# Another order for the first quarter of an attention and MoE kernel: casts with heads outermost, some joint for q and k

## The chip, the cores and the metric

The kernel runs on one core of a Trainium2 chip. The metric is device time in microseconds (us). Engines are PE (matmuls; its weight loads are listed as PEld), DVE (vector), ACT (scalar), POOL (general) and SP (which only issues transfers here). Each engine works through its instructions in the order in which they stand in its program and waits on semaphores for the others.

## The reference

Attention with a fixed mask per head, then a gated two-layer product.

```python
scores = scale * np.matmul(q, k.transpose(0, 1, 3, 2))       # 4 batches, 8 heads, 768 x 64
stream_keep = causal & (is_sink | in_win)                    # 4 sink keys, a window of 64
mask = np.where(retr[0, :, 0, 0, None, None], full_mask, stream_mask)   # heads 0, 2, 6: plainly causal
a = np.exp(scores - max);  a = a / (sum(a) + 1e-09);  attn = np.matmul(a, v)
x = attn.transpose(0, 2, 1, 3).reshape(3072, 512)
h = x @ w_in                                                 # 512 x 2048
g = h * (1.0 / (1.0 + np.exp(-beta * h)))
out = g @ w_out                                              # 2048 x 512
```

## The kernel before

The 3072 rows are worked in eight chunks of 384 rows (a batch and one of its halves), each chunk in four units of two heads: 32 units. For a unit the kernel casts k and q from float32 to bf16 (L246), turns them on PE (L326), copies them from PSUM to tiles KT and QTD (L334 for k, L337 for q), multiplies them (L455) on top of a mask that PE adds (L426), takes exp on ACT (L464), and multiplies with v (L536). v is cast into VX (L251), and the four sink keys and values go into tiles KO and VO (L316, L259, L260), both copied by POOL. DVE normalizes (L545, L549). PE turns the result (L574, copied to xT at L583), multiplies it with w_in (L604); ACT takes tanh (L609), DVE makes the gate (L612), and PE multiplies with w_out (L657).

The program's order is written out by hand. The first eight units (chunks 0 and 1) follow RAMP, a string of words that are carried out one after the other; the rest follows PLAN, likewise a string, which stands as it is. In a word the letters are the step, the number is the unit (for loads, values and rows of x: the chunk or tile), and the last letter the engine: v is DVE, a is ACT, g is POOL.

- ck, cq: the cast of k or q of a unit. tk, tq: its three transposes on PE. kk, kq: the copy to KT or QTD. ko: the sink keys.
- ad, qk, ex, ma: mask, scores, exp and mask product of a part of a unit (ex0.1 is the second part of unit 0). cv: the cast of a v tile. vo: the sink values. pv, no: the product with v and the normalization.
- xx, cx: the transposes of x and the copy to xT. hm, mm, mA: first products of the MoE part. mb: second products, four matmuls each. be: beta's transpose.
- lq, lv: loads of q and k, and of v, issued by SP (L119, L132); with a g they are held back by a small memset on POOL (L115, L129). Chunk 0's first loads are issued in front of RAMP: unit pairs 0 and 1 into one tile, 2 and 3 into another, k and q apart. wi, wo: the four loads of w_in and of w_out, issued by POOL (L140, L144). ro, rk, rq: row loads for later chunks, issued by POOL (L282).
- zz: matmuls with a tile of zeros (L517) that keep PE at work; idle(9) does the same in front of RAMP (L167).

The staging tiles of k and q and of v are two of each kind, so the loads of chunk 2 fill the tiles of chunk 0.

Of the kernel before, what the change touches and what calls it, by code (L numbers as in the profile page):

```python
# [18 lines left out]
def kernel(  # L19
# [82 lines left out]

    staged = {}

    def load_qk(c, g, pairs=1, held=False):

        b, h2 = chunks[c]
        rows = slice(h2 * HALF, (h2 + 1) * HALF)  # L110
        both = stage.tile([128, 2, 4, HT, D], F32, name=f"s{g}")
        for i, (name, src) in enumerate((("k", k), ("q", q))):
            staged[name, c, g] = both[:, i]
            if held:
                nc.gpsimd.memset(staged[name, c, g][:, 0, 0, 0:1], 0.0)  # L115
        for i in range(pairs):
            for name, src in (("k", k), ("q", q)):
                eng = nc.scalar if g == 0 and pairs == 2 and name == "q" else nc.sync
                eng.dma_start(  # L119
                    out=staged[name, c, g][:, i:4:pairs].rearrange("p h t d -> p h (t d)"),  # L120
                    in_=src[b, 4 * g + i:4 * g + 4:pairs, rows, :].rearrange("h (p t) d -> p h (t d)", t=HT))
# [20 lines left out]
    def load_w_out(i):  # L142
        f = slice(i * 4, (i + 1) * 4)
        nc.gpsimd.dma_start(out=w_out_sb[:, f, :], in_=moe_w_out.rearrange("(fo fi) d -> fi fo d", fi=128)[:, f, :])  # L144
        w_done.add(i)

    load_qk(0, 0, 2)
    load_qk(0, 1, 2)
    warm = consts.tile([1, 1], F32, name="warm")
# [7 lines left out]
    nc.vector.memset(zeros, 0.0)  # L157
# [6 lines left out]
    def idle(n, pool, name):  # L164
        for i in range(n):
            nothing = pool.tile([128, 512], F32, name=name)
            nc.tensor.matmul(nothing, zeros[:, 0:128], zeros, start=True, stop=True)  # L167
# [63 lines left out]
    def masks_late(h2):  # L231

        m = Mh[h2]
        if h2 == 0:
            return [lambda: nc.vector.tensor_copy(out=m[:, 3:5], in_=m[:, 1:3])]
        return [lambda i=i: nc.vector.tensor_copy(out=m[:, i:i + 2 * HT - 1:2], in_=Mh[0][:, i + 1:i + 2].to_broadcast([128, HT, 128]))
                for i in range(2)]


    def cast(u, name, copy):  # L240
        b, h2, p = units[u]
        c = u // NPAIR
        s = st_u.setdefault(u, {})
        if "qkb" not in s:
            s["qkb"] = att.tile([128, 2, HT, 2, D], BF16, name="qkb", bufs=4)
        copy(out=s["qkb"][:, "qk".index(name)], in_=staged[name, c, p // 2][:, p % 2:4:2].rearrange("p h t d -> p t h d"))  # L246

    def cast_v(c, t, copy):

# [39 lines left out]
    def transposes_dma(c, names=("k", "q")):  # L289
# [12 lines left out]
        for u in range(c * NPAIR, (c + 1) * NPAIR):  # L302
            p = u % NPAIR
            st_u[u] = {"QT": QT[:, place[p], :]}

    def sinks_of(u):
# [12 lines left out]
        copy(out=ko[:, ka - 1:kz - 1, 0:64], in_=kt[:, None, 0:64].to_broadcast([128, n, 64]))  # L319

    def transpose_qk(u, name):

        s = st_u.setdefault(u, {})
        tp = ps_m.tile([128, 512], F32, name="mm").bitcast(BF16)[:, 0:HALF].rearrange("p (t j) -> p t j", t=HT)
        for t in range(HT):
            nc.tensor.transpose(tp[:, t, :], s["qkb"][:, "qk".index(name), t].rearrange("p h d -> p (h d)"), ident)  # L326
        s["t" + name] = tp

    def copy_qk(u, name, copy):
# [56 lines left out]
    def steps_QK(u):  # L386
# [86 lines left out]
                        part(i)  # L473
            return (56 * sum(len(tiles[i][0]) for i in some) + 250, go)

        def mask(i):
            ev = views[i]
            ms = [[x for x, e in enumerate(tiles[i][r]) if e[5] is not None] for r in range(2)]
            if ms[0] and ms[0] == ms[1]:
                n = len(ms[0])  # L480
                m0 = tiles[i][0][0][5]
                nc.vector.tensor_mul(ev[:, :, 0:n], ev[:, :, 0:n], Mh[h2][:, None, m0:m0 + n].to_broadcast([128, 2, n, 128]))  # L482
            else:
                for r in range(2):
# [29 lines left out]
    def keep_busy(n):  # L514

        for i in range(n):
            nc.tensor.matmul(sums_bank(0), zeros[:, 0:128], zeros, start=True, stop=True)  # L517

    def steps_PV(u):
        b, h2, p = units[u]  # L520
# [180 lines left out]
    def do(word):  # L701
# [2 lines left out]
        n, i = int(n or 0), int(i or 0)  # L704
        if what in ("ck", "cq"):
            cast(n, what[1], copies[eng])
        elif what in ("tk", "tq"):
            step((170, lambda: transpose_qk(n, what[1])))
        elif what in ("kk", "kq"):
# [3 lines left out]
        elif what in ("ad", "qk", "ex", "ma"):  # L713
            if n not in visits:
                visits[n] = steps_QK(n)
            step((0 if what in ("ex", "ma") else 170, lambda: visits[n][what](i)))
        elif what == "cv":
            cast_v(n, i, copies[eng])
        elif what == "vo":
# [19 lines left out]
        elif what == "be":  # L739
            step((100, beta_go))  # L740
        elif what == "lv":
            load_v(n, held=eng == "g", tiles=[i])
        elif what == "lq":
            load_qk(n, i, held=eng == "g")
        elif what == "wi":
            load_w_in(n)
        elif what == "wo":
            load_w_out(n)
        elif what == "rq":
            rows_queries()  # L750
        elif what == "rk":
            rows_keys()
        elif what == "ro":
            if n not in more_rows:
                more_rows[n] = load_rows(n)
            more_rows[n].pop(0)()
        elif what in ("dk", "dq"):
            transposes_dma(n, what[1])
        elif what == "ml":
            late[n].pop(0)()  # L760
        elif what == "tt":
            run(steps_T(n))
        elif what == "zz":
            keep_busy(n)
        elif what == "hm":
            opened.append(done[0])
            done[0] += 1
            step(halves[0](opened[-1], 0))
        elif what == "hf":
            step(halves[0](opened.pop(0), 1))  # L770
        else:
            feed({"mm": "a", "mA": "A", "mb": "b"}[what])

    def feed(x):
# [16 lines left out]
        kq1v tk1 kk1v lq1.0g be qk0.1 ex0.0 zz3 ad1.0 cv0.0g ko1 lq1.1 ex0.1 pv0 ck3v cq3g tk3 lv1.0g cq2a tq2 kk3v  # L791
        lv1.1 cv0.1g ad1.1 qk1.1 kk2v ex1.1 tq3 ko2 qk1.0 wi0 vo0 cq4g lv1.2 cv0.2a lq2.0g ko3 pv0 kq2v pv0 ad2.0
        qk2.0 lv2.0 ex1.0 pv1 kq3a pv1 ck4v ad2.1 qk2.1 lv2.1 pv1 ex2.0 ad3.0 tq4 no0 tk4 ex2.1 ck7g kk4a qk3.0 ad3.1
        qk3.1 no1 pv2 ck6v ex3.0 cq5v ck5g pv2 tk6 xx0 ad4.0 cq6g pv3 kq4v ex3.1 pv2 ad4.1 cx0v ad5.0 qk4.1 pv3 lv2.2
        no2 on1g tq5 pv3 qk4.0 kk6a ml0 tk5 cq7g kq5v ex4.1 kk5a ko5 ko6 ad5.1 tq6 wi1 qk5.0 ex4.0 tk7 tq7 ex5.0 no3
        qk5.1 ex5.1 kq6v xx1 ad6.0 kk7v wi2 kq7v wi3 cx1a qk6.0 ml1 ad6.1 ex6.0 cv1.1g ko7 qk6.1 cv1.0v ex6.1 hm lq2.1
        ma5.0 ma5.1 mm cv1.2g vo1 mm wo0 pv4 lv3.0g ad7.0 lv3.1 pv4 hf pv4 no4 qk7.0 ad7.1 pv5 pv5 ex7.0 lv3.2 qk7.1
        pv5 no5 ml1 wo1 ex7.1 pv6 pv6 wo2 mm pv7 rq pv7 pv7 no7 wo3 pv6 no6 rk cq8g xx2 ro3 cx2a mA mA ck8g xx3 cx3a
        mm mA mm mA mm mm mA mm mm mm mA mm ro3 mm mm mA mm mm mm ro3 mA mm ro3 mA mm ro3 mm mm ro3 mA mA mb mb tt8 mb
# [116 lines left out]
```

## Time and profile before

| what | us |
|---|---|
| median of the runs shown (228.56 to 230.24) | 228.68 |
| the profiled execution's own time | 229.6 |
| its span, from the first to the last instruction | 227.7 |
| PE busy | 219.3 (96%) |
| ACT busy | 154.0 (68%) |
| DVE busy | 141.5 (62%) |
| POOL busy | 87.0 (38%) |
| the chain that ended last | PE 92% |

A row of the timeline gives the start and the length in us, the engine, the line of the kernel, the operation with output and inputs, how many instructions the row holds, and in brackets the idle time of the engine just before it with what ended it. A row of a group gives busy time and the mean duration in ns. A row of a transfer gives its size and the time from issue to landing. The profiled execution is one of several, and 0.9 us longer than the median.

### The profile page before, as it was taken

The page shows a single profiled execution, that of the slowest core. Times are in us where ns is not written, and L with a number is a line of the kernel's source. Part 1 is how long each engine was busy: PE and PEld are TensorE (multiplying, and loading weights), DVE is VectorE, ACT ScalarE, POOL GpSimd, SP SyncE. Part 2 cuts the span into 40 slices and gives each one's busy share as a digit, 9 for nine tenths or more (in the row PEclk, how much of TensorE's full clock was granted, in tenths as well). Part 3 has the DMA queues.
Part 4 walks back from the last instruction along what each step waited for, and adds up shares of the span by engine and source line. Part 5 has one row for each costly group of instructions (what it writes and reads, how often), then busy time and mean ns, then how long its engine had stood idle before and what let it go on. Part 6 is the DMA issues. An engine that isn't in the chain of part 4 may idle for free.

```text
span 227.7 us, 5023 instructions
## 1 busy us (share of the span) xinstructions
PE 219.3 (96%) x1898; PEld 126.4 (56%) x1917; DVE 141.5 (62%) x342; ACT 154.0 (68%) x254; POOL 87.0 (38%) x143
## 2 busy tenths in 40 slices
PE   7799999999999999999999999999999999999993
PEld 2456766654555665555644665556645665456553
DVE  4479988872584679347932689447964769038600
ACT  2588899846866898358943897669875877138521
POOL 5286952239254359543049209940260000000000
PEclk9999999999999999999999999999999999999998
DMA  6999999999999799989769977799804030110012
GB/s 197 233 319 239 222 197 199 194 222 165 168 207 150 176 155 113 157 191 143 96 137 147 163 173 99 90 140 153 219 4 123 8 81 0 49 62 30 0 51 91
DMA packets 95384, 31.67 MB, mean 139 GB/s; under 512 B 81776, under 2 KB 92416, under 8 KB 95360
## 3 DMA queue, kind: packets, MB, share of 16 engines
q1 hardware_dynamic: 58880, 22.82, 50.3%
q0 software_dynamic: 35904, 8.13, 41.6%
q10 hardware_dynamic: 576, 0.40, 0.6%
q8 instruction: 15, 0.25, 0.5%
q14 instruction: 9, 0.07, 0.1%
HBM read 27.27 MB, written 6.29 MB: 147 GB/s over the span
## 4 chain that ended last, share of the span: by engine, by line
PE 92%; DMA 2%; POOL 1%; ACT 1%; issue 1%; DVE 0%; SPq 0%; ACTq 0%
PE mm L657 35%; PE mm L604 25%; PE sp L604 12%; PE sp L455 7%; PE po L536 6%; DMA s<-in_k_dram 2%; PE mm L642 2%; PE mm L326 2%; PE sp L426 1%; PE mm L574 1%; PE mm L455 1%; PE mm L536 1%; DVE KT L334 0%; ACT qkb L246 0%; SPq L119 0%
## 5 line engine op out<-in xcount | busy, mean ns | idle before, releaser
L657 PE MATMUL mm<-w_out_sb,gT 128*128 128x512 bf16 x349 | 84.0, 379 | 1.3 <-issue 0.5
L464 ACT ACTIVATE es<-sp 128x768 bf16<-128x768 f32 (+2 forms) x72 | 56.5, 837 | 19.3 <-PE sp L455 19.1
L604 PE MATMUL mm<-xT,w_in_sb 128*128 128x384 bf16 x348 | 64.6, 326 | 0.0
L604 PEld LDWEIGHTS <-w_in_sb 128*128 128x128 bf16 x512 | 47.8, 98 | 29.7 <-issue 0.2
L609 ACT ACTIVATE th<-mm,beta_h 128x384 f32<-128x384 f32 x87 | 49.8, 588 | 5.8 <-PE mm L604 1.1
L657 PEld LDWEIGHTS <-gT 128*128 128x128 bf16 x368 | 33.4, 98 | 36.0 <-issue 1.5
L612 DVE SCALAR_TENSOR_TENSOR gT<-th,mm 128x384 bf16<-128x384 f32 x87 | 46.7, 551 | 6.9 <-ACT th L609 3.2
L604 PE MATMUL sp<-xT,w_in_sb 128*128 128x384 bf16 x164 | 32.3, 326 | 0.0
L251 POOL CAST VX<-vs 128x512 bf16<-128x512 f32 x16 | 10.1, 628 | 55.6 <-DMA vs<-in_v_dram 52.2
L661 ACT ACTIVATE osb<-mm 128x512 f32<-128x512 f32 x23 | 13.9, 602 | 25.5 <-PE mm L657 25.2
L536 PEld LDWEIGHTS <-es 128*128 128x128 bf16 x472 | 23.5, 98 | 12.9 <-issue 1.3
L612 DVE SCALAR_TENSOR_TENSOR gT<-th,sp 128x384 bf16<-128x384 f32 x41 | 22.3, 552 | 5.6 <-ACT th L609 3.6
L609 ACT ACTIVATE th<-sp,beta_h 128x384 f32<-128x384 f32 x41 | 23.8, 586 | 2.2 <-PE sp L604 0.2
L536 PE MATMUL po<-VX,es 128*128 128x65 bf16 x360 | 24.9, 194 | 0.4 <-ACT VX L251 0.4
L282 POOL DMA_DIRECT2D s<-in_k_dram x30 | 22.4, 757 | 7.3 <-DMA w_out_sb<-in_moe_w_out_dram 5.2
L282 POOL DMA_DIRECT2D s<-in_q_dram x30 | 22.4, 774 | 5.2 <-DMA w_out_sb<-in_moe_w_out_dram 5.2
L545 DVE RECIPROCAL rec<-po 128x6 f32<-128x6 f32 x28 | 5.4, 192 | 27.6 <-PE po L536 27.5
L455 PE MATMUL sp<-QTD,KT 64*128 64x128 bf16 (+2 forms) x258 | 19.2, 240 | 1.7 <-ACT QTD L337 1.4
L482 DVE TENSOR_TENSOR es<-es,Mh 128x768 bf16<-128x768 bf16 (+1 forms) x26 | 17.0, 683 | 5.0 <-ACT es L464 4.4
L549 DVE TENSOR_TENSOR x<-po,rec 128x384 bf16<-128x384 f32 x28 | 15.6, 557 | 1.0
L455 PEld LDWEIGHTS <-KT 64*128 64x128 bf16 x278 | 11.1, 94 | 6.9 <-issue 4.7
L259 POOL COPY VO<-VX 128x512 bf16<-128x512 bf16 x16 | 10.0, 648 | 7.4 <-DVE VX L251 7.4
(74 smaller groups left out, 157.1 us busy)
## 6 DMA issues: line engine op xcount, KB each, us to landing
vs<-in_v_dram SPq DMA_DIRECT2D x24, 256.0 KB, 5.8
out_dram<-osb SPq DMA_DIRECT2D x23, 256.0 KB, 2.8
w_in_sb<-in_moe_w_in_dram POOLq DMA_DIRECT2D x4, 512.0 KB, 9.5
w_out_sb<-in_moe_w_out_dram POOLq DMA_DIRECT2D x4, 512.0 KB, 16.6
s<-in_k_dram POOLq DMA_DIRECT2D x30, 64.0 KB, 4.3
s<-in_q_dram POOLq DMA_DIRECT2D x30, 64.0 KB, 5.9
s<-in_k_dram SPq DMA_DIRECT2D x4, 384.0 KB, 6.6
s<-in_q_dram SPq DMA_DIRECT2D x4, 384.0 KB, 8.2
```

The costliest lines, as they stand in the source:

```text
L251: copy(out=VX[b % 2][:, h2 * HT + t, :, 0:D], in_=staged["v", c][:, t])
L282: nc.gpsimd.dma_start(out=ROWS[c % 2, name][:, t, i * 4 * D:(i + 1) * 4 * D].rearrange("p (h d) -> p h d", d=D), in_=src[b, i:H:2, r:r + 1 ...
L455: nc.tensor.matmul(sps[i][r][:, x * 128:y * 128], key(a, lhs), s["QT"][half(a), qi * 128:(qi + y - x) * 128], start=first, stop=first or y ...
L464: nc.scalar.activation(out=views[i].rearrange("p r k j -> p r (k j)"), in_=banks[2][:, :, 0:n * 128], func=ACTF.Exp, scale=scale)
L482: nc.vector.tensor_mul(ev[:, :, 0:n], ev[:, :, 0:n], Mh[h2][:, None, m0:m0 + n].to_broadcast([128, 2, n, 128]))
L536: nc.tensor.matmul(po[:, qi, hh, :], e, val, start=(j == 0), stop=(j == len(lst) - 1))
L549: nc.vector.tensor_mul(xg[g][:, :, :, u % 2, :].rearrange("p a t d -> p t a d"), po[:, :, :, 0:D], rec.to_broadcast([128, HT, 2, D]))
L604: nc.tensor.matmul(hp[:, 0:HALF], w_in_sb[:, mo, fi * 128:(fi + 1) * 128], xT[c][:, mo, :], start=(mo == 0), stop=(mo == MO - 1))
L609: nc.scalar.activation(out=th, in_=hp[:, 0:HALF], func=ACTF.Tanh, scale=beta_h[:, fi:fi + 1])
L612: nc.vector.scalar_tensor_tensor(out=gTs[c][:, fi, :], in0=th, scalar=1.0, in1=hp[:, 0:HALF], op0=ALU.add, op1=ALU.mult)
L657: nc.tensor.matmul(op, gTs[c][:, fi, ns * 128:(ns + 1) * 128], w_out_sb[:, fi, :], start=(fi == 0), stop=(fi == FO - 1))
L661: nc.scalar.activation(out=osb, in_=op, func=ACTF.Copy, scale=0.5)
```

## The change

Five things change.

1. The tile of zeros is 128x128 where it was 128x512; a filler matmul streams it four times over by a broadcast. It is set first on DVE. idle(9) goes, and the word zi4 takes its place.
2. The casts of k and q read and write heads outermost; k stands ahead of q in the unit's tile.
3. cast_both casts k and q of one unit in one instruction of 768 elements per partition. Its words are cb0g, cb3a, cb4g, cb7g and cb5v, so five units use it. (Functions for transposes and copies of two units at once are defined, and no word uses them.)
4. Mask products and late masks can name an engine; the words in use leave them on DVE.
5. RAMP is another string: other engines for casts and copies, another order of loads, and another order on every engine.

```diff
-    zeros = consts.tile([128, 512], BF16, name="zeros")
+    zeros = consts.tile([128, 128], BF16, name="zeros")
+    still = zeros[:, None, :].to_broadcast([128, 4, 128])
...
-            nc.tensor.matmul(nothing, zeros[:, 0:128], zeros, start=True, stop=True)
-    idle(9, ps_m, "mm")
+            nc.tensor.matmul(nothing.rearrange("p (n j) -> p n j", n=4), zeros, still, start=True, stop=True)
...
-        copy(out=s["qkb"][:, "qk".index(name)], in_=staged[name, c, p // 2][:, p % 2:4:2].rearrange("p h t d -> p t h d"))
+        copy(out=s["qkb"][:, "kq".index(name)].rearrange("p t h d -> p h t d"), in_=staged[name, c, p // 2][:, p % 2:4:2])
...
+    def cast_both(u, copy):
+        c, p = u // NPAIR, u % NPAIR
+        s = st_u.setdefault(u, {})
+        s["qkb"] = att.tile([128, 2, HT, 2, D], BF16, name="qkb", bufs=4)
+        copy(out=s["qkb"].rearrange("p i t h d -> p i h t d"), in_=both_of[c, p // 2][:, :, p % 2:4:2])
...
     RAMP = """
-        ck0g ne1 lv0.0 lv0.1 tk0 ck2a ne0 cq0v ck1a zz3 tq0 kq0a zz3 ad0.0 on0v lv0.2 kk0v cq1v tq1 qk0.0 tk2 ad0.1
+        zi4 ad0.0 zz2 ne1 cb0g ck1a lv0.0 ne0 lv0.1 tq0 cq1g on0v tk0 lv0.2 kq0v lq1.0g zz2 kk0a tq1 tk1 ck2a qk0.0
+        ex0.0 lq1.1 ad0.1 zz5 qk0.1 be ad1.1 cb3a kk1v ex0.1 zz2 cq2a tk2 kk2v ko1 cv0.0g zz1 zz1 tk3 ad1.0 tq3
...
+        cq8g lv3.1 no5 ml1 pv6 pv6 pv6 no6 ex7.0 ex7.1 mm wo1 pv7 pv7 xx2 lv3.2 pv7 ck8g cx2a mA mA mm wo2 rq no7
```

Three places show how instructions move. The first is ACT, from its first cast on: L246 and L251 before, L248 and L312 after, are the casts (L312 the joint one), the COPY rows are those from PSUM to KT and QTD, and es is an exp. Before:

```order
L246 CAST qkb<-s_92 128x384
L246 CAST qkb<-s_87 128x384
L337 COPY QTD_144<-mm 128x384
L464 ACTIVATE es<-sp 128x768 x2
L246 CAST qkb<-s_92 128x384
L464 ACTIVATE es<-sp 128x512
L251 CAST VX_145<-vs 128x8x64
```

and after the change:

```order
L248 CAST qkb<-s_89 128x2x3x64
L361 COPY KT_131<-mm 128x384
L248 CAST qkb<-s_94 128x2x3x64
L491 ACTIVATE es<-sp 128x768
L312 CAST qkb<-s_94 128x2x2x3x64
L491 ACTIVATE es<-sp 128x768
L248 CAST qkb<-s_94 128x2x3x64
L364 COPY QTD_126<-mm 128x384
L491 ACTIVATE es<-sp 128x512
```

Unit 1's cast stands first and unit 2's third, the copy between them is that of unit 0's k, and a joint cast (unit 3, second staging tile) stands between the first two exps; the cast of a v tile is no longer ACT's.

The second place is POOL, where it issues the w_out loads, with the casts of unit 8 (staging tile s_293 before, s_312 after). Before:

```order
L251 CAST VX_146<-vs 128x8x64
L259 COPY VO_148<-VX_146 128x8x64
L260 COPY VO_148<-VX_146 4x8x64
L144 DMA w_out_sb<-in_moe_w_out_dram 128x4x512
L129 MEMSET vs 128x3
L144 DMA w_out_sb<-in_moe_w_out_dram 128x4x512 x3
L246 CAST qkb<-s_293 128x384
```

and after the change:

```order
L145 DMA w_out_sb<-in_moe_w_out_dram 128x4x512
L253 CAST VX_128<-vs 128x8x64
L130 MEMSET vs 128x3
L261 COPY VO_130<-VX_128 128x8x64
L262 COPY VO_130<-VX_128 4x8x64
L116 MEMSET s_599 128x1 x2
L248 CAST qkb<-s_312 128x2x3x64
L145 DMA w_out_sb<-in_moe_w_out_dram 128x4x512
L248 CAST qkb<-s_312 128x2x3x64
L145 DMA w_out_sb<-in_moe_w_out_dram 128x4x512 x2
```

The first w_out load moved ahead of the v cast, and the others behind the casts of unit 8: cq8g between the first and the second, ck8g between the second and the third.

The third place is SP's queue of loads, from chunk 1's v (the rows of three) to chunk 2's second half (s_293 and s_539 before, s_312 and s_599 after). Before:

```order
L132 DMA vs<-in_v_dram 128x8x64 x3
L119 DMA s_293<-in_k_dram 128x4x192
L119 DMA s_293<-in_q_dram 128x4x192
L132 DMA vs<-in_v_dram 128x8x64 x3
L119 DMA s_539<-in_k_dram 128x4x192
L119 DMA s_539<-in_q_dram 128x4x192
```

and after the change:

```order
L133 DMA vs<-in_v_dram 128x8x64 x4
L120 DMA s_312<-in_k_dram 128x4x192
L120 DMA s_312<-in_q_dram 128x4x192
L133 DMA vs<-in_v_dram 128x8x64 x3
L120 DMA s_599<-in_k_dram 128x4x192
L120 DMA s_599<-in_q_dram 128x4x192
```

One v load moved ahead of each pair of k and q.

More of the change, by code (lines that the diff above doesn't have):

```diff
@@ L145, in load_w_out @@
         w_done.add(i)
+    zeros = consts.tile([128, 128], BF16, name="zeros")
+    nc.vector.memset(zeros, 0.0)
+    still = zeros[:, None, :].to_broadcast([128, 4, 128])
     load_qk(0, 0, 2)
@@ L516, in keep_busy @@
         for i in range(n):
-            nc.tensor.matmul(sums_bank(0), zeros[:, 0:128], zeros, start=True, stop=True)
+            nc.tensor.matmul(sums_bank(0).rearrange("p (n j) -> p n j", n=4), zeros, still, start=True, stop=True)
     def steps_PV(u):
@@ L706, in do @@
             cast(n, what[1], copies[eng])
+        elif what == "cb":
+            cast_both(n, copies[eng])
+        elif what in ("wk", "wq"):
+            step((340, lambda: transpose_two(n, what[1])))
+        elif what in ("yk", "yq"):
+            copy_two(n, what[1], copies[eng])
         elif what in ("tk", "tq"):
@@ L715, in do @@
                 visits[n] = steps_QK(n)
-            step((0 if what in ("ex", "ma") else 170, lambda: visits[n][what](i)))
+            if what == "ma":
+                step((0, lambda: visits[n][what](i, engines[eng or "v"])))
+            else:
+                step((0 if what == "ex" else 170, lambda: visits[n][what](i)))
         elif what == "cv":
@@ L759, in do @@
         elif what == "ml":
-            late[n].pop(0)()
+            late[n].pop(0)(copies[eng or "v"])
         elif what == "tt":
             run(steps_T(n))
+        elif what == "zi":
+            idle(n, ps_m, "mm")
         elif what == "zz":
@@ L795 @@
[L795 to L799, printed above, removed]
@@ new lines @@
+        ko6 tk5 pv3 cx0a tq5 ex4.1 on1g no2 ad5.1 kk5a ad5.0 ko5 qk4.0 kq5a pv3 tq6 wi1 no3 qk5.0 wi2 tk7 kq6v tq7
+        qk5.1 ex4.0 ex5.0 xx1 ex5.1 kk7v ml1 kq7a ad6.0 qk6.0 hm wi3 ad6.1 ko7 cx1v wo0 qk6.1 ex6.0 ex6.1 mm ad7.0
+        cv1.1g cv1.0v ma5.1 hf pv4 ma5.v cv1.2v pv4 mm pv4 ad7.1 lv3.0g vo1 pv5 qk7.0 no4 qk7.1 pv5 rk lq2.1g pv5
+        cq8g lv3.1 no5 ml1 pv6 pv6 pv6 no6 ex7.0 ex7.1 mm wo1 pv7 pv7 xx2 lv3.2 pv7 ck8g cx2a mA mA mm wo2 rq no7
+        xx3 mA cx3v wo3 mm ro3 mm mm mA mm mm mm mA mA mm mm mA ro3 mm mm mA ro3 mm mm ro3 mm mA mm ro3 mm mm ro3 mA
@@ L801 @@
+        mA mb mb tt8 mb mb mb
     """
```

44 lines of the change are left out of this document (29 added, 15 removed).

## The prediction

> **What bounds the kernel now.** I read the page's shares and chain first, then the busy time by stretch, then the rows of single engines.
>
> ```profile
> PE 219.3 (96%) x1898; PEld 126.4 (56%) x1917; DVE 141.5 (62%) x342; ACT 154.0 (68%) x254; POOL 87.0 (38%) x143
> PE 92%; DMA 2%; POOL 1%; ACT 1%; issue 1%; DVE 0%; SPq 0%; ACTq 0%
> 0.00:5.00 5.00, 3.71 (x12) 1.33 (x13) 1.86 (x8) 1.49 (x2) 3.25 (x15) 1.00 0.59 179
> 20.00:25.00 5.00, 4.96 (x54) 2.98 (x55) 4.87 (x9) 5.00 (x8) 4.89 (x10) 1.00 1.21 243
> 30.00:50.00 20.00, 19.95 (x125) 11.74 (x124) 16.37 (x31) 16.48 (x29) 7.34 (x11) 1.00 1.25 202
> ```
>
> The columns of a stretch are its length, then the busy time of PE, PEld, DVE, ACT and POOL, and behind them the granted clock (1.00). From 30 to 50 us PE is busy 19.95 of 20 and the chain is 92% PE: behind the ramp the kernel is a row of matmuls, and the change leaves these in place. So a gain can come only from the first 25 us, and only if PE reaches the same matmul sooner. In 20 to 25 us PE, DVE, ACT and POOL are all nearly full, ACT with 5.00 of 5. The PE waits of that part:
>
> ```profile
> 1.29 3.59 PE L167 MATMUL mm<-zeros 128*128 128x512 bf16 x9 [1.29 <-DVE zeros L157]
> 5.02 0.81 PE L517 MATMUL po<-zeros 128*128 128x512 bf16 x3
> L517 PE MATMUL po<-zeros 128*128 128x512 bf16 x9 | 2.4, 380 | 0.0
> 8.46 0.34 PE L455 MATMUL sp<-QTD,KT 64*128 64x128 bf16 x4 [1.40 <-ACT QTD L337]
> 13.18 0.31 PE L536 MATMUL po<-VX,es 128*128 128x65 bf16 x5 [0.40 <-ACT VX L251]
> 15.40 0.34 PEld L326 LDWEIGHTS <-qkb 128*128 128x128 bf16 x6 [0.34 <-POOL s L115]
> 20.04 0.34 PE L455 MATMUL sp<-QTD,KT 64*128 64x256 bf16 x4 [0.25 <-ACT KT L334]
> ```
>
> The largest is 1.40 us ahead of the first scores at 8.46; the three behind it add 0.40 + 0.34 + 0.25 = 0.99. That is all the named waiting there is to win: 2.39 us, 1.0% of the time. (About 1% is what a measurement of this kernel can tell from no change.)
>
> **The start.** What releases the first scores now:
>
> ```profile
> 7.11 0.92 ACT L246 CAST qkb<-s 128x384 bf16<-128x384 f32 x2 [3.74 <-DMA s<-in_k_dram]
> 7.94 0.47 ACT L337 COPY QTD<-mm 128x384 bf16<-128x384 bf16 x1
> 8.84 0.81 ACT L464 ACTIVATE es<-sp 128x768 bf16<-128x768 f32 x1 [0.43 <-PE sp L455]
> 9.94 0.81 ACT L464 ACTIVATE es<-sp 128x768 bf16<-128x768 f32 x1 [0.29 <-PE sp L455]
> 3.93 0.41 POOL L187 TENSOR_SCALAR_AFFINE_SELECT Nc<-Nc 128x256 bf16<-128x256 bf16 x1
> s<-in_q_dram SPq DMA_DIRECT2D x1, 192.0 KB, 5.0
> L246 POOL CAST qkb<-s 128x384 bf16<-128x384 f32 x8 | 4.1, 525 | 2.2 <-PE sp L604 1.4 <-PE mm L326 0.4 <-DMA s<-in_q_dram 0.3
> L246 ACT CAST qkb<-s 128x384 bf16<-128x384 f32 x3 | 1.4, 507 | 3.7 <-DMA s<-in_k_dram 3.7
> L251 POOL CAST VX<-vs 128x512 bf16<-128x512 f32 x4 | 2.5, 628 | 5.3 <-DMA vs<-in_v_dram 5.3
> L251 ACT CAST VX<-vs 128x512 bf16<-128x512 f32 x1 | 0.6, 612 | 0.0
> ```
>
> Before, ACT takes unit 2's cast ck2a first, whose k lands at about 7.1; behind it stand the cast of unit 1 and kq0a, the copy that the first scores need. The change puts kq0 on DVE, and unit 0's k and q into one POOL cast of 768 elements. No row shows such a cast. From 384 elements in 525 ns and 512 in 628 ns, an element more costs 0.80 ns, so I take 628 + 256 x 0.80 = 833 ns; the same step on ACT (507 and 612) gives 822. The ends: no shorter than the 628 of 512 elements, no longer than two single casts, 1,050. POOL is free at 3.93 + 0.41 = 4.34, so cb0g ends at about 5.2, the copies kq0v and kk0a follow the transposes, and I put the first scores at about 6.65: 1.8 us earlier than 8.46.
>
> Almost none of that lasts. The first exp (L464) now stands behind ck2a, whose data still land at 7.1, so it starts at 7.1 + 0.5 = 7.6 instead of 8.84. Next on ACT is cb3a, the joint cast of unit 3: it waits for **both** loads, and the q of that pair is issued at 3.95 and lands 5.0 later, at 8.95. It runs 8.95 to 9.8, and ex0.1 stands behind it. ex0.1 starts at 9.7, where it started at 9.94. The head start of 1.8 is 0.2 at this point; the five fillers (zz5) ahead of its scores lie in the same wait and cost nothing.
>
> **From 10 to 24 us: ACT.** Between ex0.1 and the first tanh at about 24 the two orders differ on ACT as follows:
>
> ```profile
> L337 ACT COPY QTD<-mm 128x384 bf16<-128x384 bf16 x2 | 1.0, 476 | 0.0
> 12.02 0.60 ACT L464 ACTIVATE es<-sp 128x512 bf16<-128x512 f32 x1 [0.88 <-PE sp L455]
> 15.96 0.48 ACT L334 COPY KT<-mm 128x384 bf16<-128x384 bf16 x1 [0.33 <-PE mm L326]
> 18.45 0.81 ACT L464 ACTIVATE es<-sp 128x768 bf16<-128x768 f32 x1 [0.44 <-PE sp L455]
> 23.83 1.23 ACT L609 ACTIVATE th<-mm,beta_h 128x384 f32<-128x384 f32 x2
> ```
>
> Gone are cv0.2a (0.61) and kk6a (0.48); new are kq1a, kq5a and kq7a (3 x 0.48 = 1.44); cx1a and cx0a are the same work. ACT gets 1.44 - 1.09 = 0.35 us **more** to do and starts it 0.2 earlier. If its idle time stays where it is, the first tanh comes 0.15 later. Its larger idle times in between were 0.88 + 0.33 + 0.44 = 1.65. If all of that closed up, the tanh would come 1.5 earlier. I take the first end, nearer to the rows, because landings still hold the middle:
>
> ```profile
> s<-in_q_dram SPq DMA_DIRECT2D x1, 384.0 KB, 4.9
> 15.30 0.13 POOL L115 MEMSET s<- 128x1 f32 x2
> ```
>
> Chunk 1's q is issued at 9.86 and lands 4.9 later, at 14.75, whatever stands ahead. Before, k and q of unit 4 were cast apart and POOL's half was done at 15.3 (the memset that follows it); the joint cb4g starts at 14.75 and takes 0.83, so tq4, at 15.41 before, starts at about 15.6 or 15.7: 0.25 later. The wait at 13.18 for the third value tile goes, since cv0.2 moves to the DVE, but what it won is waited for at tq4. I carry **+0.1** to the first tanh and from there to the end; ends -1.5 and +0.35.
>
> Costed at nothing: heads outermost in the casts on ACT and POOL (same elements) and DVE (off the path, since kk and kq copies follow by PE's transposes); the narrow zero tile (the matmul streams the same 512 columns); fillers, which fill waits. Should a filler stand where PE no longer waits it costs (0.81 - 0.38) / 2 = 0.215 each (the row of 5.02 and the mean of its group, 380 ns), four of them 0.9. cv1.2 on the DVE behind mask products takes the value copies of POOL with it; it frees 0.63 of POOL, and stays inside the full stretch of DVE, at most 0.45 later.
>
> **The weights.** This is the one place where the change adds a wait in front of a queue. POOL issues the four w_out loads one behind the other; afterwards the cast cq8g stands between the first and the second, and it needs the q of chunk 2, which SP now issues behind one more v load.
>
> ```profile
> 25.42 0.75 POOL L144 DMA_DIRECT2D w_out_sb<-in_moe_w_out_dram  x1
> 26.19 2.24 POOL L144 DMA_DIRECT2D w_out_sb<-in_moe_w_out_dram  x3
> 29.88 0.51 POOL L246 CAST qkb<-s 128x384 bf16<-128x384 f32 x1 [1.45 <-PE sp L604]
> w_out_sb<-in_moe_w_out_dram POOLq DMA_DIRECT2D x1, 512.0 KB, 12.7
> w_out_sb<-in_moe_w_out_dram POOLq DMA_DIRECT2D x1, 512.0 KB, 20.6
> 19.54 2.01 SPq L119 DMA_DIRECT2D s<-in_q_dram  x1
> s<-in_q_dram SPq DMA_DIRECT2D x1, 384.0 KB, 10.2
> vs<-in_v_dram SPq DMA_DIRECT2D x1, 256.0 KB, 14.7
> w_in_sb<-in_moe_w_in_dram POOLq DMA_DIRECT2D x1, 512.0 KB, 8.8
> 48.91 1.46 PE L657 MATMUL mm<-w_out_sb,gT 128*128 128x512 bf16 x6
> ```
>
> Before, that q landed at 19.54 + 10.2 = 29.7 and the v load behind it (issued 21.65) at 36.35. Exchanged, the two together still end at about 36.3, so cq8g runs at 36.3 to 36.8 and the second w_out load is issued at 36.8 instead of 26.2. The first one lands at 25.42 + 12.7 = 38.1, the fourth at 27.66 + 20.6 = 48.3, so one takes 3.4 us while the queue is full. Up to 38.1 nothing is lost; then the queue is dry until the second load's packets come. How long that is no row shows apart: the first w_in load, into an empty queue, took 8.8 from issue to landing, so at most 8.8 - 3.4 = 5.4 went by before its data flowed, and at least none. With 5.4 the dry time is 36.8 + 5.4 - 38.1 = 4.1, with none 0. I take 2, the middle. The fourth load then lands at 50.3. PE needs it at the fourth group of second products: 48.91 + 4 x 0.216 = 49.8 (spacing from the six of that row). That is a wait of 0.5, of which the row loads of chunk 3, next in POOL's queue, may add a little. Because the packets of SP's queue run faster while POOL's is dry, I take **+0.2**; ends 0 and 2.6.
>
> **Sum.** 0.1 + 0.2 = +0.3. The profiled execution took 229.6 (span 227.7 and 1.9 around it), so it would be 229.9; the median of the runs shown is 228.68, 0.9 below that execution, so I forecast 229.0.
>
> **Rivals.** *A, the head start survives.* ACT closes its idle time and PE's waits at 13.18, 15.40 and 20.04 go: 228.7 - 1.5 = 227.2. For it speaks that they are ACT's waits for PE; against it that q lands at 14.75 in both. More than 1% would take all 2.39 us of waits.
>
> *B, PE's clock comes up later.* Before, nine fillers ran from 1.29 to 4.88, and PE was fast at 5.02 (0.215 a filler).
>
> ```profile
> 3.40 0.15 PEld L167 LDWEIGHTS <-zeros 128*128 128x128 bf16 x1 [0.28 <-issue]
> ```
>
> Until then one came every 0.15 + 0.28 = 0.43 us. Now only four stand there, to about 3.0, and the next matmuls wait for Nc until 4.34. The granted clock reads 1.00 from 0 to 5 us too, so that column doesn't show the difference. If the slow rate lasts to the first scores, these stand at about 8.1 (4 fillers and 12 transposes later than 6.65 by 1.5, if each takes twice its time), still no later than before, but the five fillers behind them cost 5 x 0.215 = 1.1 more, of which 0.2 to 0.6 is hidden in the wait for cb3a: 229.0 + 0.8 = 229.8. The Trainium skill ("TensorE: Matmul & The Clock Gate", Part 1) says that the array runs at half rate until it was busy through a free-running window of about 3.4 us; by that rule the gap at 3.0 to 4.3 can cost a second slow window, and the time would be that of B. The spacing of the fillers agrees with a halved rate.
>
> *C, slower: the w_out queue runs dry for long.* Place: cq8g between the first and second w_out load. It decides from the point at which the fourth load lands behind 49.8, that is from a dry time of 1.5 us on; each us more is a us of PE waiting. At the end of 4.1 it is 228.7 + 0.1 + 2.6 = 231.4. For it: POOL runs in order and cq8g cannot pass. Against: a later load by SP means less traffic beside the weights.
>
> *D, nothing moves:* the ramp is reshuffled inside landings, 228.7; it lies in the forecast's own range.
>
> **How the numbers follow.** Forecast with D 0.50, A 0.15, B 0.12, C 0.23. The likeliest case spans 228.2 to 229.6. The range reaches to A (227.2) below and to C's end above, 231.4. Faster by over 1% (under 226.4) needs more than A's 1.5: 0.07. Slower by over 1% (over 231.0) needs C near its end, or C and B: 0.18. Within 1%: 0.75.
>
> **What would show it.** First scores near 6.65; ex0.1 no earlier than 9.6, with cb3a ending the wait for a q load; tq4 at 15.6; first tanh at 23.9 to 24.1. The second w_out load issued at about 37, directly behind cq8g, and a PE wait of about half a microsecond on w_out near 50. Wrong would be: scores at 8 or later (B), a tanh before 23 (A), w_out landing after 52 (C), or a wait behind 55 us that this list does not have.

## The result, and the profile after

The changed kernel takes 230.69 us (median of 8 runs, 229.63 to 231.4), the kernel before 228.8 (228.52 to 230.24). The ratio is 1.0074, 95% interval 1.0051 to 1.0096: slower by 0.7%. The profiled executions hide this. That of before took 229.6, 0.8 over its median, and that of after 229.63, 1.1 **under** its median; their spans are 227.7 and 227.8. Whoever compares only the two pages sees no difference. So the changed kernel was profiled once more, below, in an execution that took 2.2 longer than the median of its set. Ratios here and below compare executions in the chip's fast state; of the changed kernel's thirteen, one of 236.12 us was in the slow one and is left out of its ratio.

The page of the first profile after, busy time by engine, and the chain:

```profile
PE 221.1 (97%) x1916; PEld 127.5 (56%) x1916; DVE 138.3 (61%) x339; ACT 154.7 (68%) x255; POOL 86.9 (38%) x142
PE 95%; ACT 1%; POOL 1%; issue 0%; DVE 0%; POOLq 0%; ACTq 0%
```

It is still a row of matmuls. Its start, PE's timeline (L170 and L544 are the zero matmuls, L453 the masks, L353 the transposes of k and q, L482 the scores):

```profile
1.06 1.89 PE L170 MATMUL mm<-zeros 128*128 128x512 bf16 x4 [1.06 <-DVE warm L155]
4.39 0.37 PE L453 MATMUL sp<-Nc,idb 128*128 128x128 bf16 x2 [1.44 <-POOL Nc L189]
5.41 0.84 PE L353 MATMUL mm<-idb,qkb 128*128 128x128 bf16 x6
7.68 0.50 PE L482 MATMUL sp<-QTD,KT 64*128 64x128 bf16 x4
8.52 1.56 PE L544 MATMUL po<-zeros 128*128 128x512 bf16 x5
16.03 0.50 PE L353 MATMUL mm<-idb,qkb 128*128 128x128 bf16 x6
```

Six transposes take 0.84 us at 5.41 and 0.50 at 16.03: PE runs at half its rate until about 9.3, inside the row of five zero matmuls. The first scores stand at 7.68. Before they stood at 8.46, so a head start of 0.8 is there. ACT behind it (L491 is exp, L312 a joint cast, L636 tanh):

```profile
8.22 0.81 ACT L491 ACTIVATE es<-sp 128x768 bf16<-128x768 f32 x1 [1.04 <-PE sp L482]
8.93 0.82 ACT L312 CAST qkb<-s 128x768 bf16<-128x768 f32 x1
10.40 0.81 ACT L491 ACTIVATE es<-sp 128x768 bf16<-128x768 f32 x1 [0.64 <-PE sp L482]
24.26 1.22 ACT L636 ACTIVATE th<-mm,beta_h 128x384 f32<-128x384 f32 x2
```

The second exp comes at 10.40, later than the 9.94 of before, and it waited for PE. The first tanh comes at 24.26 (before 23.83). Now the w_out loads, from POOL's timeline (L248 is the cast of k or q, here cq8g), the landing of the fourth (issued at 35.14) and PE's second products (L684):

```profile
32.77 0.50 POOL L248 CAST qkb<-s 128x384 bf16<-128x384 f32 x1 [6.58 <-DMA s<-in_q_dram]
33.22 0.75 POOL L145 DMA_DIRECT2D w_out_sb<-in_moe_w_out_dram  x1
34.41 1.49 POOL L145 DMA_DIRECT2D w_out_sb<-in_moe_w_out_dram  x2
w_out_sb<-in_moe_w_out_dram POOLq DMA_DIRECT2D x1, 512.0 KB, 14.7
49.04 3.18 PE L684 MATMUL mm<-w_out_sb,gT 128*128 128x512 bf16 x14
```

cq8g waited 6.58 us for q of chunk 2, and the fourth load, issued at 35.14, landed at 49.8. PE needs it four matmuls into the row at 49.04, at 49.9: in this execution it was just in time.

### The profile page after: what moved, and what is told of

Same layout as the page of the kernel before. It is cut to its first block, busy times and chain, and to the rows that moved or that the text cites. A ratio compares the mean times of both kernels' runs of the same rounds, so it can differ in the third digit from the quotient of the medians.

```text
span 227.8 us, 5036 instructions
## 1 busy us (share of the span) xinstructions
PE 221.1 (97%) x1916; PEld 127.5 (56%) x1916; DVE 138.3 (61%) x339; ACT 154.7 (68%) x255; POOL 86.9 (38%) x142
## 4 chain that ended last, share of the span: by engine, by line
PE 95%; ACT 1%; POOL 1%; issue 0%; DVE 0%; POOLq 0%; ACTq 0%
PE mm L684 35%; PE mm L631 25%; PE sp L631 12%; PE sp L482 7%; PE po L563 6%; PE mm L353 2%; PE sp L453 2%; PE po L544 2%; PE mm L669 2%; PE mm L601 1%; PE mm L482 1%; ACT es L491 1%; PE mm L563 1%; POOL Mh L173 0%; ACT QTD L364 0%
## 5 line engine op out<-in xcount | busy, mean ns | idle before, releaser
L684 PE MATMUL mm<-w_out_sb,gT 128*128 128x512 bf16 x368 | 85.9, 379 | 0.0
L491 ACT ACTIVATE es<-sp 128x768 bf16<-128x768 f32 (+2 forms) x72 | 56.6, 838 | 20.6 <-PE sp L482 20.3
L631 PE MATMUL mm<-xT,w_in_sb 128*128 128x384 bf16 x348 | 64.8, 326 | 0.0
L631 PEld LDWEIGHTS <-w_in_sb 128*128 128x128 bf16 x512 | 47.7, 98 | 29.8 <-issue 0.3
L684 PEld LDWEIGHTS <-gT 128*128 128x128 bf16 x368 | 33.4, 98 | 36.0 <-issue 1.5
L636 ACT ACTIVATE th<-mm,beta_h 128x384 f32<-128x384 f32 x87 | 49.7, 587 | 5.6 <-PE mm L631 0.7
L631 PE MATMUL sp<-xT,w_in_sb 128*128 128x384 bf16 x164 | 32.1, 326 | 0.0
L253 POOL CAST VX<-vs 128x512 bf16<-128x512 f32 x15 | 9.8, 653 | 48.3 <-DMA vs<-in_v_dram 44.9
L636 ACT ACTIVATE th<-sp,beta_h 128x384 f32<-128x384 f32 x41 | 23.8, 586 | 2.7 <-DVE xT L610 0.4
L482 PE MATMUL sp<-QTD,KT 64*128 64x128 bf16 (+2 forms) x258 | 19.3, 242 | 0.1
L509 DVE TENSOR_TENSOR es<-es,Mh 128x768 bf16<-128x768 bf16 (+1 forms) x26 | 14.3, 578 | 5.0 <-ACT es L491 4.4
L576 DVE TENSOR_TENSOR x<-po,rec 128x384 bf16<-128x384 f32 x28 | 15.6, 557 | 1.0
L482 PEld LDWEIGHTS <-KT 64*128 64x128 bf16 x278 | 11.1, 94 | 5.7 <-issue 3.9
```

Of the source, the lines that this page charges most:

```text
L482: nc.tensor.matmul(sps[i][r][:, x * 128:y * 128], key(a, lhs), s["QT"][half(a), qi * 128:(qi + y - x) * 128], start=first, stop=first or y ...
L491: nc.scalar.activation(out=views[i].rearrange("p r k j -> p r (k j)"), in_=banks[2][:, :, 0:n * 128], func=ACTF.Exp, scale=scale)
L509: eng.tensor_mul(ev[:, :, 0:n], ev[:, :, 0:n], Mh[h2][:, None, m0:m0 + n].to_broadcast([128, 2, n, 128]))
L576: nc.vector.tensor_mul(xg[g][:, :, :, u % 2, :].rearrange("p a t d -> p t a d"), po[:, :, :, 0:D], rec.to_broadcast([128, HT, 2, D]))
L631: nc.tensor.matmul(hp[:, 0:HALF], w_in_sb[:, mo, fi * 128:(fi + 1) * 128], xT[c][:, mo, :], start=(mo == 0), stop=(mo == MO - 1))
L636: nc.scalar.activation(out=th, in_=hp[:, 0:HALF], func=ACTF.Tanh, scale=beta_h[:, fi:fi + 1])
```

## The experiments

**The changed kernel again**, nothing edited.

> The changed kernel, once more, for a second profile. The first one took 229.63 us, 1.06 under the median of its runs, 230.69, so what makes the usual run longer isn't in it. Clock theory (PE stays at half rate until a point that differs from run to run; in the first profile until about 9.3 us): a profile near 230.7 shows the last 0.43 us spacing of zero matmuls, or transposes of 0.84 us per six, later than 9.3 by up to 2 us, and the first tanh about 1 us later than 24.26. Transfer theory (landings differ from run to run): the same loads land later than in the first profile (k of the second pair of units at 5.8, its last q at 7.70), and PE waits for them.

Median 231.18 of five, ratio 1.0086 (1.0069 to 1.0102). This profile took 233.4 us. PE's timeline, POOL's (L631 are the first products), the q of chunk 2 (issued 22.20), the fourth w_out load (issued 38.06), and the stretch of 50 to 55 us (length, busy time of PE, PEld, DVE, ACT and POOL, granted clock):

```profile
8.34 1.24 PE L544 MATMUL po<-zeros 128*128 128x512 bf16 x5
48.55 1.03 PE L684 MATMUL mm<-w_out_sb,gT 128*128 128x512 bf16 x4
51.85 4.44 PE L684 MATMUL mm<-w_out_sb,gT 128*128 128x512 bf16 x12 [2.28 <-DMA w_out_sb<-in_moe_w_out_dram]
35.70 0.50 POOL L248 CAST qkb<-s 128x384 bf16<-128x384 f32 x1 [9.80 <-PE mm L631]
s<-in_q_dram SPq DMA_DIRECT2D x1, 384.0 KB, 13.4
w_out_sb<-in_moe_w_out_dram POOLq DMA_DIRECT2D x1, 512.0 KB, 13.7
50.00:55.00 5.00, 3.15 (x9) 1.17 (x9) 0.08 (x1) 1.00 (x2) 2.85 (x5) 0.75 1.60 164
```

Neither theory that was written ahead fits: the clock came up at about 8.1, earlier than in the first profile, and though the first loads landed a microsecond later (the last q of chunk 0 at 8.7 against 7.7), the second products began earlier, at 46.48 against 46.98. The loss lies at 50 us: cq8g ran at 35.70, just behind the landing at 35.6 of the q that it reads (the row puts the wait down to a first product, which it does not read), the fourth w_out load landed at 51.8, and PE waited **2.28 us** for it. Rival C's mechanism, at C's price. In this execution the wait then costs a second time: behind it twelve matmuls take 4.44 us, where 14 took 3.18 above, and the granted clock of that stretch is 0.75.

**Eight zero matmuls at the start.**

```diff
-        zi4 ad0.0 zz2
+        zi8 ad0.0 zz2
```

> The changed kernel with eight zero matmuls at its start instead of four, so that PE works from 1.06 us without a break to the masks (ready at about 4.4 us). Clock theory: the full rate comes at about 5 us as in the kernel before, six transposes take 0.51 instead of 0.84, the five fillers 1.25 instead of 1.56, ex0.1 starts at about 9.3 instead of 10.40, and the time falls by 0.8 to 1.8 us against the changed kernel, to about 229 to 229.9. Rival (ACT and the landings set the ramp, the clock is hidden): no change, 230.7.

231.43, ratio 1.0114 (1.0080 to 1.0147): not faster, although the ramp did what the clock theory said, if not as early as it said.

```profile
6.70 0.50 PE L353 MATMUL mm<-idb,qkb 128*128 128x128 bf16 x6
46.22 1.89 PE L684 MATMUL mm<-w_out_sb,gT 128*128 128x512 bf16 x7
52.31 3.61 PE L684 MATMUL mm<-w_out_sb,gT 128*128 128x512 bf16 x16 [2.64 <-DMA w_out_sb<-in_moe_w_out_dram]
```

The full rate is there at 6.70 and the second products begin at 46.22 instead of 46.98 or 46.48, and all of it is waited away at 52.31. A gain ahead of a late load is worth nothing; the two causes have to be taken apart.

**The kernel before with four zero matmuls instead of nine.**

```diff
-    idle(9, ps_m, "mm")
+    idle(4, ps_m, "mm")
```

> The kernel before with four zero matmuls at its start instead of nine; PE then idles from about 3 to 4.8 us. Clock theory: the half rate lasts until 8 to 9 us, the scores of unit 0 and the fillers behind them are late, and it loses 0.3 to 1.5 us: 229.1 to 230.3. Rival (its first scores wait for a k load and two casts on ACT until 8.46 us, which hides a slow PE): 228.8, no change.

230.12, ratio 1.0060 (1.0039 to 1.0081): slower by 1.4 us, as the clock theory had it.

```profile
4.84 0.50 PE L326 MATMUL mm<-idb,qkb 128*128 128x128 bf16 x3 [1.66 <-POOL s L115]
5.14 1.48 PE L517 MATMUL po<-zeros 128*128 128x512 bf16 x3
8.69 0.34 PE L455 MATMUL sp<-QTD,KT 64*128 64x128 bf16 x4
```

Three zero matmuls take 1.48 us where they took 0.81, and no wait stands ahead of the scores any more: the half rate itself sets them. So the zero matmuls at the start are not idle work in the kernel before.

**All four w_out loads where the first is.**

```diff
-        ... ko7 cx1v wo0 qk6.1 ...
+        ... ko7 cx1v wo0 wo1 wo2 wo3 qk6.1 ...
```

> The changed kernel with all four w_out loads issued together, where the first stands now, ahead of the cast that waits for q of chunk 2. Weights theory (the fourth w_out load lands at 49.80 us where PE needs it at 49.91, so that PE waits in every run that is a little less lucky): 0.3 to 1 us faster than the changed kernel, 229.7 to 230.4. Clock theory: no change, 230.7; the fourth load then lands two or more us before it is needed, and nothing is gained.

231.35, ratio 1.0104 (1.0088 to 1.0121). The wait at 50 is gone, another has taken its place (L253 is the cast of v):

```profile
22.52 2.97 POOL L145 DMA_DIRECT2D w_out_sb<-in_moe_w_out_dram  x4
26.16 0.25 PE L563 MATMUL po<-VX,es 128*128 128x65 bf16 x3 [1.62 <-POOL VX L253]
```

Issuing four loads holds POOL for 2.97 us, and the v cast behind them makes PE wait 1.62. So the forecast of the weights theory did not come, yet this doesn't speak against it, since the edit put a new wait in the place of the old one.

**The three loads behind the sink values and ahead of cq8g.** The words wo1, wo2 and wo3 leave their places:

```diff
-        cq8g lv3.1 no5 ...
+        wo1 wo2 wo3 cq8g lv3.1 no5 ...
```

> The changed kernel with the second, third and fourth w_out loads moved ahead of the cast cq8g, behind the sink value copies of chunk 1. Weights theory (cq8g waits until 32.8 to 35.7 us for q of chunk 2, the loads behind it land up to 2.3 us later than PE needs the fourth, and how much later differs from run to run): the fourth lands near 48.3 us, no wait for w_out near 50 us, and the median falls to 229.3 to 229.8, what the one lucky profile of the changed kernel took. Rival (the usual run loses elsewhere, in the ramp's clock or landings): 230.7 or more, as the changed kernel.

229.34, ratio 1.0024 (1.0005 to 1.0042), inside the weights theory's range.

```profile
25.45 2.22 POOL L145 DMA_DIRECT2D w_out_sb<-in_moe_w_out_dram  x3
w_out_sb<-in_moe_w_out_dram POOLq DMA_DIRECT2D x1, 512.0 KB, 21.3
48.23 4.48 PE L684 MATMUL mm<-w_out_sb,gT 128*128 128x512 bf16 x20
```

The fourth load, issued at 26.91, landed at 48.3; twenty second products run in 4.48 us without a gap. Against the two ratios of the unedited kernel that is 0.0050 to 0.0062 less, **1.1 to 1.4 us**: the larger part of the loss.

**The load order alone.** SP issues the first v load of chunk 2 behind that chunk's k and q again; the w_out loads stay behind the casts.

```diff
-        ex1.0 kk3v lv2.0 cb4g pv0 lq2.0g pv1
+        ex1.0 kk3v cb4g pv0 lq2.0g lv2.0 pv1
```

> The changed kernel with one load moved: SP issues the first v load of chunk 2 behind that chunk's first k and q, as the kernel before does; the w_out loads stay behind cq8g and ck8g. Weights theory: that q lands at about 30 us, cq8g ends by 31, the second w_out load is issued long before the first lands at 38, and the median is 229.3 to 229.8 as with the loads moved. If the place behind the casts alone does it: 230.7 or more.

229.53, ratio 1.0017 (0.9995 to 1.0039): the same gain. POOL's timeline:

```profile
27.99 0.52 POOL L248 CAST qkb<-s 128x384 bf16<-128x384 f32 x1
28.44 1.48 POOL L145 DMA_DIRECT2D w_out_sb<-in_moe_w_out_dram  x2
```

The casts of unit 8 are through by 28.5. So in the changed kernel it takes both edits to do the harm: the loads behind the cast, and the cast's data behind one more load.

**Both edits in the kernel before.** v load of chunk 2 ahead of its k and q, w_out loads two to four behind the casts of unit 8.

```diff
-        ... cq4g lv1.2 cv0.2a lq2.0g ko3 ... ad2.0 qk2.0 lv2.0 ex1.0 ...
+        ... cq4g lv1.2 cv0.2a lv2.0 lq2.0g ko3 ... ad2.0 qk2.0 ex1.0 ...
...
-        ... wo1 ex7.1 pv6 pv6 wo2 ... no7 wo3 pv6 no6 rk cq8g xx2 ro3 cx2a mA mA ck8g xx3
+        ... ex7.1 pv6 pv6 ... no7 pv6 no6 rk cq8g wo1 xx2 cx2a mA mA ck8g wo2 wo3 ro3 xx3
```

> The kernel before with only that pair of edits: the first v load of chunk 2 ahead of its k and q, and the w_out loads two to four behind the casts of unit 8 as in the changed kernel. Weights theory: the fourth w_out load lands at 50 to 52.5 us, PE waits for it near 50, and the time rises by 0.5 to 2.5 us, to 229.4 to 231.4. Rival: 228.9.

231.48, ratio 1.0111 (1.0073 to 1.0149): 2.5 us slower, by this pair alone, the upper end of what was expected.

```profile
34.61 0.50 POOL L246 CAST qkb<-s 128x384 bf16<-128x384 f32 x1 [8.58 <-DMA s<-in_q_dram]
50.77 1.46 PE L657 MATMUL mm<-w_out_sb,gT 128*128 128x512 bf16 x6 [1.83 <-DMA w_out_sb<-in_moe_w_out_dram]
7.57 0.34 PE L455 MATMUL sp<-QTD,KT 64*128 64x128 bf16 x4
45.85 1.89 PE L657 MATMUL mm<-w_out_sb,gT 128*128 128x512 bf16 x7
```

POOL waits 8.58 us, between the 6.58 and 9.80 of the changed kernel, and PE 1.83. The profile shows something else: up to there this is the ramp of before, and its first scores stand at 7.57 and its second products at 45.85, both about a microsecond earlier than in the profile that the prediction was made from. The last q of chunk 0 landed at 8.0 here and at 9.0 there.

**The w_out loads ahead and eight zero matmuls.**

> The same with eight zero matmuls at the start instead of four. Clock theory beside the weights theory: the first second product comes at about 46.2 us instead of 46.5 to 47.0, and with the weights in time that is kept: 228.6 to 229.2, level with the kernel before. Rival (the clock's delay is hidden): the same time as with four.

228.75, ratio 0.9994 (0.9980 to 1.0007): level with the kernel before. Against the same with four zero matmuls that is 0.0030, or **0.7 us**, for the clock, with intervals that do not meet the other's middle. The runs also scatter less: 228.36 to 229.36, with four 228.69 to 230.82.

From this kernel on, three edits to the ramp and one to a cast. **Without the five zero matmuls between the first scores:**

```diff
-        ex0.0 lq1.1 ad0.1 zz5 qk0.1 be ...
+        ex0.0 lq1.1 ad0.1 qk0.1 be ...
```

> The changed kernel with the w_out loads ahead of cq8g and eight zero matmuls at the start (228.75 us), and now without the five zero matmuls between the first and the second scores of unit 0. Filler theory (they delay beta's transpose, behind which stand on DVE the k copy of unit 1, and behind that on POOL its sink keys and the first v cast, which starts at 10.57 us though its tile landed at 9.19): beta's product comes at about 8.5 instead of 9.63 on DVE, the v cast at about 9.5, and the time falls by 0.3 to 0.9 us, to 227.9 to 228.5. Rival (as forecast, the five lie in the wait for the joint cast cb3a and cost nothing): 228.75.

228.68, ratio 0.9985 (0.9966 to 1.0003). The v cast came at 9.54 instead of 10.57, ex0.1 at 9.27 instead of 9.48, and the time did not move by more than the measurement tells: the forecast's "cost nothing" held.

**Beta's scaling behind the k copy of unit 1:**

```diff
-        ... be ad1.1 cb3a kk1v ex0.1 ...
+        ... ad1.1 cb3a kk1v be ex0.1 ...
```

> The same starting point, with the five fillers kept and beta's scaling moved behind the k copy of unit 1 on DVE (and its transpose on PE with it). Filler theory: the k copy starts at about 7.6 instead of 9.73 us, the sink keys and the v cast follow at 9.2; if the v cast sets the ramp, 0.2 to 0.6 us are gained. Rival: 228.75, since PE's own row of matmuls sets the pace there.

228.57, ratio 0.9984 (0.9970 to 0.9999), the lowest of all versions, but barely to be told from the kernel before, and not from the version that it started from (0.9994). **Both, and four more zero matmuls left out:**

```diff
-        ... zz5 qk0.1 be ad1.1 cb3a kk1v ex0.1 zz2 cq2a tk2 kk2v ko1 cv0.0g zz1 zz1 tk3
+        ... qk0.1 ad1.1 cb3a kk1v be ex0.1 cq2a tk2 kk2v ko1 cv0.0g tk3
```

> Both, and the four fillers behind the second scores of unit 0 (two ahead of and two behind the transposes of unit 2) left out too, so nine fewer. Filler theory: PE runs up against the exps and landings instead, the ramp is 0.5 to 1.2 us shorter, 227.5 to 228.3. Rival (the ramp is held by ACT and by the q of chunk 1, landing at about 14): 228.75; and if PE falls back to the half rate in the gaps, more than 229.

228.76, ratio 0.9994 (0.9974 to 1.0015): no gain, so the filler theory's 0.5 to 1.2 us did not come. PE's timeline of the version with beta moved (first four rows), and of the last one (fifth):

```profile
5.15 0.51 PE L353 MATMUL mm<-idb,qkb 128*128 128x128 bf16 x6
6.40 0.34 PE L482 MATMUL sp<-QTD,KT 64*128 64x128 bf16 x4
12.76 0.27 PE L453 MATMUL sp<-Ns,idb 128*128 128x256 bf16 x1 [0.44 <-ACT es L491]
14.76 0.51 PE L353 MATMUL mm<-idb,qkb 128*128 128x128 bf16 x6 [0.41 <-POOL s L116]
15.38 0.51 PE L353 MATMUL mm<-idb,qkb 128*128 128x128 bf16 x6 [0.80 <-POOL s L116]
```

In that execution PE was at full rate at 5.15 and the first scores stood at 6.40. What was won is waited for at unit 4's transposes (14.76), behind the joint cast of a q that landed at 13.74; with nine fillers fewer the wait there is 0.80 (its q landed at 14.35), not a shorter ramp. The 0.44 at 12.76 is a wait for an exp. **That joint cast taken apart:**

```diff
-        ex1.0 kk3v lv2.0 cb4g pv0
+        ex1.0 kk3v lv2.0 ck4v cq4g pv0
```

> The kernel with the w_out loads early, eight zero matmuls and beta moved (228.57 us), and now with unit 4's joint cast taken apart: k on DVE as soon as it lands (about 12.5 us), q on POOL, as the kernel before casts it. Landing theory (unit 4's transposes stand at 14.76 us behind a q that lands at 13.74, and the joint cast adds 0.82 behind that landing where a single one adds 0.51): they start 0.3 us earlier and the time falls by 0.2 to 0.3, to 228.3. ACT theory (the exps from there on are back to back, the transposes don't matter): 228.57, no change.

228.73, ratio 0.9985 (0.9969 to 1.0002): no difference to the joint one that these runs can tell. The wait ahead of the transposes is gone from its profile, and the next exps are as full as before: ACT's theory, though a fifth of a microsecond could hide in the interval.

**All the profiles together.** Take from the time of each profiled execution the start of its second products, as in these rows of the kernel before (229.6 us) and of the first profile after (229.63 us):

```profile
46.85 1.89 PE L657 MATMUL mm<-w_out_sb,gT 128*128 128x512 bf16 x7
46.98 1.89 PE L684 MATMUL mm<-w_out_sb,gT 128*128 128x512 bf16 x8
```

What is left is 182.6 to 182.9 us in all eleven executions in which PE did not wait for w_out. In the three in which it did, it is 186.9, 185.8 and 184.6, with waits of 2.28, 2.85 (0.21 and 2.64) and 1.83; the first has the half rate behind its wait. So these versions differ in two places alone, the start of the second products and the wait for w_out.

## Why the prediction was right, and where it was not

The forecast was 229.0 against 228.68, "+0.3"; measured are 1.7 us by the ratio of the first comparison and 2.0 by the second. Direction, range and "within 1%" held, the range because it reached up to C's end. The sum itself did not hold, nor did the likeliest case, whose own range ended at 229.6. What happened is rivals B and C together: 0.7 for the clock and 1.1 to 1.4 for the weights are 1.8 to 2.1, the whole of what was measured.

- **What bounds the kernel** held: matmuls from 30 us on, and a gain only by reaching the same matmul sooner. (That about 1% is what a measurement can tell was too cautious: these intervals are a quarter of a per cent to either side, or less, for the unedited kernel.)
- **The joint cast** at 0.83: 0.82 on ACT and 0.82 to 0.95 on POOL.
- **First scores at 6.65.** Measured 7.68, and 6.40 where PE was at full rate. The step that failed is that the transposes and fillers were counted at full rate; their doubled cost, which rival B put at 1.5, is what is missing; between these two executions it is 1.28.
- **The head start is lost to landings.** Right in kind, wrong in the first place named. cb3a did not wait for its q: that landed 3.7 us after its issue at 4.01, not 5.0, and cb3a ran at 8.93 directly behind the exp. ex0.1 came at 10.40 and 9.90 (forecast 9.7), held by PE's half rate, and at 9.48 with eight zero matmuls at the start and the loads ahead. The second place, unit 4's transposes behind the joint cast, came out in number alone: forecast 15.6, measured 16.03 and 15.53. But the q did not hold it there. It was issued earlier than before and had landed at 13.65 and 14.42, and the cast began at 15.10 and 14.60, directly behind POOL's copies of the values. The wait for the q shows only when the ramp is faster (row 14.76 above).

```profile
s<-in_q_dram SPq DMA_DIRECT2D x1, 192.0 KB, 3.7
```

- **ACT, +0.1.** First tanh forecast at 23.9 to 24.1; measured 24.26 and 23.76. But the profile of before that it was measured against was an execution with late landings. In the one with the kernel before's ramp and earlier landings the first tanh is at 23.01:

```profile
23.01 1.23 ACT L609 ACTIVATE th<-mm,beta_h 128x384 f32<-128x384 f32 x2
```

  so the loss of the ramp in those two executions is 0.75 to 1.25, of which the clock is 0.7 by the medians. With the clock mended the second products come at 46.06 against 45.85 in single executions, +0.2, and by the medians (0.9994) nothing is left: the term's +0.1 cannot be told from either.
- **Rival B, "229.8", that is +0.8 beside the forecast**: measured 0.7. Its size was right, its chance of 0.12 too small. Its sign, scores at 8 or later, did not come (7.68). The gap at 3.0 to 4.4 us was seen and its consequence written down. In the traces of the changed kernel's start with four zero matmuls the full rate came at about 7, 7.5, 8.1, 9.3 and 10 us in five executions, with eight at 4.1 to 7.1 in six. The Trainium skill ("TensorE: Matmul & The Clock Gate", Part 1) has the array at half rate until a free-running window of about 3.4 us was busy. The varying moment and the later rise behind a gap agree with that; but in the execution with 7 only 2.7 us had passed since PE took up work again at 4.38, so such a window cannot have been busy throughout.
- **The weights, +0.2, ends 0 and 2.6.** The mis-sized term. Measured 1.1 to 1.4 in the median and 2.28 of wait in one execution. The chain of the step was right link by link, as far as PE's wait: q of chunk 2 behind the v load (landing at 32.7 and 35.6, forecast 36.3), cq8g behind it, the second load issued at 33.2 and 36.15 (forecast 36.8), the fourth landing at 49.8 and 51.8 (forecast 50.3). The dry time, put at 2, was 2.3 in the second profile (first landing at 38.2, second at 43.9, less 3.4) and 0.7 in the first. What was missing: the two later loads took about 4 us each instead of 3.4 (38.06 + 13.7 = 51.8, less the second's landing at 36.15 + 7.7 = 43.9, is 7.9 for two; in the first profile it is 7.1); PE was there a little earlier than the late profile said (48.55 + 4 x 0.216 = 49.4 against 49.8); and a wait of that length can bring the half rate back. The deduction from 0.5 to 0.2 for faster packets on SP's queue had no row behind it and should not have been made. Its premise does show in the second profile, where three v loads landed at 38.7, 39.7 and 41.1, about 1 us apart, against 6.8 and 5.6 before; but that brings no w_out load earlier.

```profile
w_out_sb<-in_moe_w_out_dram POOLq DMA_DIRECT2D x1, 512.0 KB, 7.7
```

- **Costed at nothing**: the fillers held, by the run without five of them. The heads-outermost casts and the narrow zero tile were not tried alone; since the kernel with both mended is level with before, they cost no more than the interval together with the new order; what each does alone stays open. On DVE the casts of 384 elements did get shorter, 411 ns on average against 543.
- **Rival A** did not come: even with clock and weights mended the ramp gives 0.9994, and with beta moved 0.9984.

## What to carry to other kernels

A cast that waits for a transfer does not belong ahead of load issues on the same engine: the wait is passed on to every load behind it, and is paid much later, where those loads are needed. A profile of before is one execution; if it took 0.8 us more than the median, find what was late in it (here the first landings) before terms of 0.1 are summed on its rows. Filler matmuls at the start are to be judged by when the rows show the full rate, not by whether their time lies in a wait.

## What the runs showed of the hardware that was not expected

A wait of 2.28 us on PE in the middle of the kernel was followed by matmuls at half rate (12 in 4.44 us), while waits of 2.64 and 1.83 us in two other executions were not (16 in 3.61 us behind the first). The stretches behind the wait of 2.28, with the granted clock third from the end of each row:

```profile
52.00:53.00 1.00, 1.00 (x5) 0.42 (x4) 0.00 (x0) 0.00 (x0) 0.91 (x2) 0.75 1.76 157
53.00:54.00 1.00, 1.00 (x4) 0.35 (x3) 0.00 (x0) 0.86 (x2) 1.00 (x3) 0.50 1.67 159
54.00:55.00 1.00, 1.00 (x3) 0.30 (x2) 0.00 (x0) 0.14 (x1) 0.94 (x3) 0.50 1.60 159
55.00:56.00 1.00, 1.00 (x4) 0.42 (x3) 0.00 (x0) 0.00 (x0) 1.00 (x1) 0.54 1.86 154
```

From 56 us on it is 1.00 again. The first matmuls behind the wait, from 51.85, still ran at the full rate; the half rate lasted 0.5 + 1 + 1 + 0.9 = 3.4 us and cost 1.7. The Trainium skill ("TensorE: Matmul & The Clock Gate", Part 1) puts the return to half rate after at least one idle window of about 3.4 us, free-running. The length of the half-rate stretch agrees with such a window, but a wait of 2.28 us is shorter than one, so here the figure is no safe limit for a gap. Why the longer wait of 2.64 was not followed by it stays open. A granted clock under 0.995 over the whole execution was measured in kernels with this wait alone (0.990, 0.993 and 0.989, at 233.3 to 233.6 us).

The same first loads, in the same order, landed about a microsecond apart from one execution to another: the last q of the first chunk took 5.0 us in the profile of before, 3.7 and 4.5 in the two of the changed kernel. What makes them differ stays open.
